# Dealing the second batch's side work at .56 of the feed-forward's work instead of .6 in the first sweep

## The chip, the core and the metric

One core of a Trainium2 chip runs the whole program. The engines named below are TensorE (PE, matmuls and transposes; PEld is its weight load), VectorE (DVE), ScalarE (ACT), GpSimd (POOL) and the SyncE queue (SP), which issues most transfers. The metric is the device time of one execution in microseconds (us), as the median of the runs shown.

## The reference

Attention on 8 batches of 12 heads, 448 tokens and 64 columns, then a spectral mixing of the 448 x 768 result, then a feed-forward network with 3072 hidden columns:

```python
q_n, k_n = (rmsnorm(q, g_q), rmsnorm(k, g_k))
scores = scale * np.matmul(q_n, k_n.transpose(0, 1, 3, 2))
attn = np.exp(scores - np.max(scores, axis=-1, keepdims=True))
attn = attn / (np.sum(attn, axis=-1, keepdims=True) + 1e-09)
x = np.matmul(attn, v)            # heads side by side: 448 x 768
mixed = np.real(np.fft.fft(np.fft.fft(x, axis=1), axis=2))
u = x + mixed
un = (u - mu) / np.sqrt(var + 1e-06)
out = u + np.maximum(un @ w_ch1, 0.0) @ w_ch2
```

The two weight matrices come in as 64-bit floating point numbers.

## The kernel before

The kernel makes 8 **sweeps**, one for each batch b. A sweep is the feed-forward of batch b, `ffn(b, ...)`, on TensorE: 24 pieces `up(m)` that make `h_m` (18 matmuls of 128x448 each, three passes on a high and a low half for precision), evacuated by ACT (high half) and DVE (low half) into `hs_m`, and 36 pieces `down(g, d)` that make `o_g_d` (12 matmuls each), added by DVE into `acc`. The order is `up(0)`, then for each group g of six four `up` and six `down`. The matmuls of both write to two banks of PSUM (`ffn`), so each piece waits until the piece two before it has been evacuated. It gives back its cost in nominal ns after each piece (3420 for an `up`, 2280 for a `down`).

While batch b is in the feed-forward, the **side work** of batch b+1 is dealt between the pieces: `aux(b + 1)`, a generator that gives attention (six head pairs: scores `S`, softmax `P`, transposes `pt`, products `av`), then the folds of its result for the Fourier transform (`fold`: DVE adds into `eo`, `sd`, `tot`), then `spectral`: matmuls `y`, evacuated to `Y`, matmuls `ab`, combined into `smdf`, then four token tiles, made in the order `un_0`, `un_2`, `un_1`, `un_3`: for each two groups of transposes (`x_000`, `x_001` for `un_0`, `x_010`, `x_011` for `un_2`, `x_10.` for `un_1`, `x_11.` for `un_3`; they take turns on two banks), a DVE pass to `u` with a sum `st`, an ACT pass to the centred rows `un` and an ACT pass that squares them (`xr`). At the start of the next sweep `ffn_input` transposes those four tiles into the six inputs `unT_0` to `unT_5` (PE transposes `un_p<-ident,un_i`, ACT high half, DVE low half), which `up(0)` needs.

`merge` sets how fast the side work is dealt:

```python
for cost in main:
    done += cost
    while side_done < done * ratio:
        x = next(side, None)
        ...
        side_done += x
```

with `RATIO = 0.49` in the sweeps from the second on and `RATIO_FIRST` in the first, where b is 0 and the side work is that of batch 1. The feed-forward of a sweep gives back 24 x 3420 + 36 x 2280 = 164160 in all.

The first sweep has a third load: the weights. There each piece's weights are loaded as 64-bit words (`dbl`), turned into two 32-bit halves by ACT, DVE and POOL (`mag`, lines 783 to 797, `w`, lines 802 and 803), and written back for the later sweeps, which only load them. A scheduler then sets the order of each engine's instructions from this program order and its own estimate of times; each engine runs its own list strictly in order.

Of the kernel before, what the change touches and what calls it, by code (L numbers as in the profile page):

```python
# [37 lines left out]


RATIO = 0.49  # L40
RATIO_FIRST = 0.6
CONVERT_EARLY = 0.12
EARLY = 2
DFT_STEP = 40
# [47 lines left out]
def spectral_block(ctx, tc, q, k, v, g_q, g_k, w1, w2, d1, d2, out, nb=B):  # L92
# [663 lines left out]
    def aux(b):  # L756

        EO, uns[b] = [], {}
        yield from attention(b, EO)
        yield from spectral(b, xTs[b], EO, uns[b])  # L760
# [368 lines left out]
    for b in range(nb):  # L1129
        merge(  # L1130
            ffn(b, ffn_input(b, uns.pop(b))),
            second if b == 0 else aux(b + 1) if b + 1 < nb else iter(()),
            RATIO if b else RATIO_FIRST,
        )
# [24 lines left out]
```

## Time and profile before

| | |
|---|---|
| time before, median of 3 runs | 2141.39 us (2141.15 to 2144.48) |
| profiled execution: time | 2144.78 us |
| profiled execution: span of the core | 2143.0 us |
| mean granted TensorE clock, of full speed | 0.984 |
| PE busy | 2074.9 us (97%) |
| DVE busy | 1548.4 us (72%) |
| ACT busy | 1023.3 us (48%) |
| POOL busy | 342.1 us (16%) |
| sweep 0, from its first matmul `h_0` | 177.0 us |
| sweep 1, from its first matmul `h_0` | 455.59 us |

The profiled execution took 3.39 us more than the median, so a sum of differences is made against its rows and then set on the median. Busy time of PE counts matmuls that overlap; what PE loses is read from its waits and from the granted clock, PEclk (1.00 is 2.4 GHz, 0.50 is 1.2 GHz). Sweep 0 runs from 177 to 455 us; before it stands the first batch's side work.

### The profile page before, as it was taken

Reading aid. Unit: us, or ns where it says so; the run is one execution under the profiler, and the core shown is the slowest. Engines: PE = TensorE matmul, PEld = TensorE weight load, DVE = VectorE, ACT = ScalarE, POOL = GpSimd, SP = SyncE. Lnnn points to the kernel's source line nnn. Section 1 sums busy time; section 2 is a strip of 40 time slices with the busy share of each in tenths; the row PEclk is TensorE's granted clock in tenths of the full one; section 3 lists DMA queues with packets and bytes.
Section 4 is the critical chain, followed back from the end, with each engine's and each line's share of the span. In section 5 each row is a group of like instructions: output and inputs, shape, how many; then the busy total and the mean of one; then the engine's idle time right before and its main releaser. Section 6 shows DMA issues by size and latency. Waiting matters only on the chain.

```text
span 2143.0 us, 31181 instructions
## 1 busy us (share of the span) xinstructions
PE 2074.9 (97%) x11256; PEld 1846.7 (86%) x11256; DVE 1548.4 (72%) x2948; ACT 1023.3 (48%) x2182; POOL 342.1 (16%) x182
## 2 busy tenths in 40 slices
PE   7877999999999999999999999999999999999998
PEld 4546888889999999999999999999999989999998
DVE  6788888977885878757886778858787578764122
ACT  6857876446542555335542455425553455422100
POOL 3324433311110101001110111101010011000000
PEclk9987999999999999999999999999999999999999
DMA  6538876776566855658555765667556674458874
GB/s 185 184 97 297 275 263 220 269 237 189 174 180 189 235 165 174 187 183 231 156 175 176 240 181 169 179 194 229 166 177 189 190 206 138 152 174 253 233 251 150
DMA packets 283550, 423.86 MB, mean 198 GB/s; under 512 B 181075, under 2 KB 200516, under 8 KB 283396
## 3 DMA queue, kind: packets, MB, share of 16 engines
q1 hardware_dynamic: 278962, 419.75, 63.8%
q10 hardware_dynamic: 4434, 2.11, 0.4%
q8 instruction: 90, 1.47, 0.3%
q14 instruction: 64, 0.52, 0.1%
HBM read 362.01 MB, written 65.31 MB: 199 GB/s over the span
## 4 chain that ended last, share of the span: by engine, by line
PE 81%; DVE 6%; DMA 5%; ACT 3%; issue 2%; POOL 1%; SPq 1%; DVEq 0%; POOLq 0%; ACTq 0%
PE h L1039 29%; PE o L1060 29%; PE S L409 5%; PE av L521 4%; PE pt L509 4%; DMA dbl<-w 2%; PE y L646 2%; PE qk L345 1%; DMA w<-w 1%; PE av L483 1%; DMA ur<-u_dram 1%; ACT P L115 1%; PE oT L996 1%; PE x L677 1%; PE un L908 1%
## 5 line engine op out<-in xcount | busy, mean ns | idle before, releaser
L1039 PE MATMUL h<-unT,w 128*128 128x448 f32 x3456 | 792.0, 372 | 3.4 <-DVE unT L115 1.4
L1060 PE MATMUL o<-hs,w 128*128 128x448 f32 x3456 | 786.4, 371 | 3.1 <-DVE acc L115 1.5
L1039 PEld LDWEIGHTS h<-unT,w 128*128 128x128 f32 x3456 | 638.9, 189 | 57.8 <-DVE unT L115 1.7
L1060 PEld LDWEIGHTS o<-hs,w 128*128 128x128 f32 x3456 | 635.9, 188 | 58.6 <-issue 3.4
L115 ACT ACTIVATE P<-S,mn 112x448 f32<-112x448 f32 x384 | 244.1, 638 | 232.6 <-DVE mn L115 226.7
L115 DVE TENSOR_REDUCE mn<-S 112x1 f32<-112x448 f32 x384 | 232.8, 616 | 47.9 <-PE S L409 38.3
L115 ACT ACTIVATE hs<-h 128x448 fp32r<-128x448 f32 x192 | 104.2, 543 | 299.0 <-PE h L1039 298.2
L115 DVE TENSOR_TENSOR acc<-o,acc 128x448 f32<-128x448 f32 (+1 forms) x240 | 146.9, 614 | 126.6 <-PE o L1060 125.0
L115 DVE SCALAR_TENSOR_TENSOR hs<-h,hs 128x448 fp32r<-128x448 f32 x192 | 119.0, 620 | 139.7 <-ACT hs L115 138.6
L115 POOL TENSOR_TENSOR qkn<-raw 112x1024 f32<-112x1024 f32 x36 | 68.6, 1904 | 679.3 <-PE qk L345 606.1
L115 POOL TENSOR_TENSOR ss<-ss,nhalf 112x16 f32<-112x16 f32 x48 | 142.6, 2972 | 190.2 <-DVE ss L115 167.2
L115 ACT CAST T<-pt 128x448 fp32r<-128x448 f32 x216 | 113.2, 532 | 107.3 <-PE pt L509 105.0
L521 PE MATMUL av<-T,vhl 128*128 128x448 f32 x432 | 151.0, 382 | 0.0
L115 DVE TENSOR_TENSOR T<-pt,T 128x448 fp32r<-128x448 f32 x216 | 131.4, 616 | 25.8 <-ACT T L115 24.7
L115 DVE TENSOR_SCALAR P<-P,sm 112x448 f32<-112x448 f32 x288 | 126.6, 479 | 3.8
L409 PE MATMUL S<-KD,QT 128*112 128x448 f32 x328 | 126.5, 386 | 0.6 <-ACT P L115 0.5
L509 PE MATMUL pt<-ident,P 112*128 112x112 f32 x864 | 124.8, 259 | 0.0
L409 PE MATMUL S<-rounded,QT 128*112 128x448 f32 x328 | 119.9, 366 | 0.0
L509 PEld LDWEIGHTS pt<-ident,P 112*128 112x128 f32 x864 | 103.5, 140 | 16.3 <-DVE R L115 0.3
L115 POOL TENSOR_TENSOR rstd<-st,nhalf 112x1 f32<-112x1 f32 (+2 forms) x32 | 20.2, 632 | 507.7 <-DVE st L115 507.7
L797 POOL TENSOR_TENSOR mag<-mag,dbl 128x768 uint32<-128x768 uint32 (+1 forms) x33 | 75.9, 2301 | 140.6 <-DVE mag L793 93.5
L521 PEld LDWEIGHTS av<-T,vhl 128*128 128x128 f32 x432 | 80.9, 188 | 8.3
(120 smaller groups left out, 2501.4 us busy)
## 6 DMA issues: line engine op xcount, KB each, us to landing
w<-w SPq DMA_DIRECT2D x192, 768.0 KB, 4.9
w<-w SPq DMA_DIRECT2D x288, 512.0 KB, 4.4
dbl<-w SPq DMA_DIRECT2D x20, 768.0 KB, 4.7
dbl<-w SPq DMA_DIRECT2D x13, 1024.0 KB
raw<-q SPq DMA_DIRECT2D x96, 112.0 KB, 3.8
raw<-k SPq DMA_DIRECT2D x96, 112.0 KB, 4.6
values<-v SPq DMA_DIRECT2D x96, 96.0 KB, 4.2
u_dram<-u SPq DMA_DIRECT2D x24, 336.0 KB, 3.8
```

The costliest lines, as they stand in the source:

```text
L115: ins = emit(*args, **kwargs)
L345: nc.tensor.transpose(pt[:, c * C : (c + 1) * C], qk[:, i, c].rearrange("t h d -> t (h d)"), ident[:C, :C],)
L409: ins = nc.tensor.matmul(s_, QT[:, h, cs], K[:, h], start=step == 0, stop=step == 1)
L483: nc.tensor.matmul(av[:, :S], vhl[:, 3 * h + j].rearrange("s h d -> s (h d)"), T, start=h + j == 0, stop=False,)
L509: nc.tensor.transpose(pt[:, c * C : (c + 1) * C], Pc[c][:, 512 * h + j * 128 : 512 * h + (j + 1) * 128], ident[:C, :C],)
L521: nc.tensor.matmul(av[:, :S], lv, T[:, i], start=(j == 0 and i == 0), stop=False)
L646: nc.tensor.matmul(o, src[:, par, t0 : t0 + n], D1[:, ri, par, cols], start=i != 1, stop=i != 0,)
L677: nc.tensor.transpose(xp[:n, i * 128 : (i + 1) * 128], src[:, 3 * half + i], ident)
L797: behind(nc.gpsimd.tensor_tensor(out=bits, in0=bits, in1=low, op=ALU.add))
L908: nc.tensor.transpose(pt[:, OFFS[i] : OFFS[i] + LENS[i]], uns[i][:, p * 128 : (p + 1) * 128], ident[: LENS[i], : LENS[i]],)
L1039: pace(nc.tensor.matmul(o, w[:, a, c], unT[c][:, z], start=n == 0, stop=n == 17))
L1060: pace(nc.tensor.matmul(o, w[:, a, f], hs[4 * g + f][:, z], start=n == 0, stop=n == 11))
```

## The change

One number: in the first sweep the second batch's side work is dealt until it has reached .56 of the feed-forward's work so far, instead of .6.

```diff
-RATIO_FIRST = 0.6
+RATIO_FIRST = 0.56
```

No instruction of arithmetic is added or taken away; what moves is the place of side work in the lists of the engines, between about 185 and 550 us of the trace. Three places show it.

**PE, at the end of sweep 0, before.** The rows are the transposes `x_110` and `x_111` (from the attention result `xT`) that start the last token tile, the `down` pieces `o_5_3` and `o_5_4`, and transposes of the feed-forward input (`un_1_4211<-ident,un_2_3932` is tile `un_2` for the input `unT_1`):

```order
L677 MATMUL x_110_4028<-ident,xT_1698 112x128 x3
L677 MATMUL x_111_4033<-ident,xT_1698 112x128 x3
L1060 MATMUL o_5_3_4155<-hs_23_4100,w_0_5_3_4022 128x448 x2
L908 MATMUL un_1_4211<-ident,un_1_3994 128x112
L908 MATMUL un_1_4211<-ident,un_2_3932 128x111
L908 MATMUL un_3_4227<-ident,un_1_3994 128x112
L908 MATMUL un_3_4227<-ident,un_2_3932 128x111
L1060 MATMUL o_5_4_4171<-hs_20_3707,w_0_5_4_4068 128x448 x3
```

A little further down the same list, the last `down` piece, the transposes of the last token tile, here `un_3_4040`, the next batch's scores and sweep 1's first matmul:

```order
L1060 MATMUL o_5_5_4187<-hs_21_4019,w_0_5_5_4103 128x448 x3
L1060 MATMUL o_5_5_4187<-hs_22_4065,w_0_5_5_4103 128x448 x3
L1060 MATMUL o_5_5_4187<-hs_23_4100,w_0_5_5_4103 128x448 x3
L908 MATMUL un_0_4203<-ident,un_3_4040 128x112
L908 MATMUL un_1_4211<-ident,un_3_4040 128x112
L908 MATMUL un_2_4219<-ident,un_3_4040 128x112
L908 MATMUL un_3_4227<-ident,un_3_4040 128x112
L409 MATMUL S_0_1_0_4312<-KD_0_3299,QT_0_3298 112x448
L409 MATMUL S_0_1_0_4312<-rounded,QT_0_3298 112x448
L409 MATMUL S_0_1_1_4313<-KD_0_3299,QT_0_3298 112x448
L409 MATMUL S_0_1_1_4313<-rounded,QT_0_3298 112x448
L1039 MATMUL h_0_4268<-unT_0_4208,w_1_0_4121 128x448
```

**The same place after the change**, from the last rows of `o_5_5` on; the transposes `x_100` to `x_111` that start the last two token tiles stand here:

```order
L1060 MATMUL o_5_5_4187<-hs_23_4045,w_0_5_5_4048 128x448 x3
L409 MATMUL S_0_0_0_4295<-KD_0_3353,QT_0_3352 112x448
L409 MATMUL S_0_0_0_4295<-rounded,QT_0_3352 112x448
L409 MATMUL S_0_0_1_4296<-KD_0_3353,QT_0_3352 112x448
L409 MATMUL S_0_0_1_4296<-rounded,QT_0_3352 112x448
L677 MATMUL x_100_4069<-ident,xr_1_4067 112x128 x3
L677 MATMUL x_101_4074<-ident,xr_1_4067 112x128 x3
L677 MATMUL x_110_4105<-ident,xT_1698 112x128 x3
L677 MATMUL x_111_4110<-ident,xT_1698 112x128 x3
L908 MATMUL un_0_4203<-ident,un_0_3999 128x113
L908 MATMUL un_0_4203<-ident,un_1_4081 128x112
L908 MATMUL un_0_4203<-ident,un_2_4020 128x111
```

and the rows that follow a little later, the transposes of the last token tile, now `un_3_4117`, up to sweep 1's first matmul:

```order
L908 MATMUL un_0_4203<-ident,un_3_4117 128x112
L908 MATMUL un_1_4211<-ident,un_3_4117 128x112
L908 MATMUL un_2_4219<-ident,un_3_4117 128x112
L908 MATMUL un_3_4227<-ident,un_3_4117 128x112
L409 MATMUL S_0_1_0_4312<-KD_0_3353,QT_0_3352 112x448
L409 MATMUL S_0_1_0_4312<-rounded,QT_0_3352 112x448
L409 MATMUL S_0_1_1_4313<-KD_0_3353,QT_0_3352 112x448
L409 MATMUL S_0_1_1_4313<-rounded,QT_0_3352 112x448
L1039 MATMUL h_0_4268<-unT_0_4208,w_1_0_4101 128x448
```

The `x_11.` transposes moved from the middle of `o_5_3` to behind `o_5_5`, and with them those of `x_10.`, which stood between `o_5_1` and `o_5_2`; between `x_111` and the transposes of the last tile `un_3` there were two whole `down` pieces (24 matmuls), and now there is none.

**PE, where the spectral part begins, before.** The matmuls `y` stood behind the first `down` of group 4:

```order
L1060 MATMUL o_4_0_3714<-hs_19_3648,w_0_4_0_3507 128x448 x3
L646 MATMUL y_0_0_3741<-D_76,eo_0_3408 113x2x65
L646 MATMUL y_0_1_3778<-D_76,eo_0_3408 112x2x65
L646 MATMUL y_1_0_3788<-D_76,eo_0_3408 113x2x65
L646 MATMUL y_1_1_3825<-D_76,eo_0_3408 112x2x65
L646 MATMUL y_0_0_3741<-D_76,eo_1_3579 113x2x65
```

After the change they stand behind `h_22`:

```order
L1039 MATMUL h_22_3933<-unT_5_1657,w_0_22_3731 128x448 x3
L646 MATMUL y_0_0_3840<-D_76,eo_0_3489 113x2x65
L646 MATMUL y_0_1_3877<-D_76,eo_0_3489 112x2x65
L646 MATMUL y_1_0_3913<-D_76,eo_0_3489 113x2x65
L646 MATMUL y_1_1_3923<-D_76,eo_0_3489 112x2x65
L646 MATMUL y_0_0_3840<-D_76,eo_1_3638 113x2x65
```

The first `y` matmuls moved past five `down` pieces and two `up` pieces; the first transposes of the first token tile (`un_0`), which stood just ahead of `h_23`, moved behind `o_5_3`.

**DVE, the third fold**, before. The rows are the fold of the last three head pairs (`eo_2`, `sd_2`, then into `eo_0`, `eo_1`, `tot`), with evacuations `hs` and weight conversion (`mag`, `w`) between:

```order
L115 TENSOR_TENSOR eo_2_3678<-xT_1698 128x449 x2
L115 TENSOR_TENSOR sd_2_3677<-eo_2_3678 128x2x225 x2
L115 TENSOR_TENSOR eo_2_3678<-sd_2_3677 128x4x113
L115 SCALAR_TENSOR_TENSOR hs_19_3648<-h_19_3629,hs_19_3648 128x448
L115 TENSOR_TENSOR eo_2_3678<-sd_2_3677 128x4x112
L803 TENSOR_TENSOR w_0_4_4_3651<-mag_4_4_3652,w_0_4_4_3651 128x512
L785 TENSOR_SCALAR mag_22_3766<-mag_22_3766 128x768
L115 SCALAR_TENSOR_TENSOR eo_0_3408<-eo_2_3678,eo_0_3408 128x900
L115 TENSOR_TENSOR eo_1_3579<-eo_1_3579,eo_2_3678 128x900
L115 TENSOR_TENSOR tot_3586<-tot_3586,eo_2_3678 128x900
```

and after the change, from its second step on, beside the evacuations of `o_4_4` and `o_4_5`:

```order
L115 TENSOR_TENSOR acc_1660<-o_4_4_3822,acc_1660 128x448
L803 TENSOR_TENSOR w_0_5_1_3836<-mag_5_0_3810,w_0_5_1_3836 128x512
L115 TENSOR_TENSOR sd_2_3757<-eo_2_3758 128x2x225 x2
L115 TENSOR_TENSOR acc_1660<-o_4_5_3850,acc_1660 128x448
L785 TENSOR_SCALAR mag_5_4_3956<-mag_5_4_3956 128x1024
L115 TENSOR_TENSOR eo_2_3758<-sd_2_3757 128x4x113
L115 TENSOR_TENSOR eo_2_3758<-sd_2_3757 128x4x112
L803 TENSOR_TENSOR w_0_5_2_3864<-mag_5_2_3865,w_0_5_2_3864 128x512
L789 TENSOR_SCALAR mag_5_4_3956<-mag_5_4_3956 128x1024
L115 SCALAR_TENSOR_TENSOR eo_0_3489<-eo_2_3758,eo_0_3489 128x900
L115 TENSOR_TENSOR eo_1_3638<-eo_1_3638,eo_2_3758 128x900
L115 TENSOR_TENSOR tot_3645<-tot_3645,eo_2_3758 128x900
```

The fold moved from `h_19` to the end of `down` group 4 and the start of `h_21`, and the last weights (`w_0_5_.`) are now converted between its steps.

## Rows read from the trace of the kernel before

**Rows 1.** Groups of the page: busy us, mean ns | idle us before.
```profile
L115 DVE TENSOR_REDUCE mn<-S 112x1 f32<-112x448 f32 x384 | 232.8, 616 | 47.9 <-PE S L409 38.3
...
L115 DVE TENSOR_SCALAR P<-P,sm 112x448 f32<-112x448 f32 x288 | 126.6, 479 | 3.8
```

**Rows 2.** Windows of sweep 0: length, busy us by engine, PEclk, DMA.
```profile
177.00:356.50 179.50, 175.65 (x892) 147.57 (x893) 152.52 (x226) 137.85 (x260) 70.29 (x35) 0.98 0.82 276
356.50:439.00 82.50, 76.30 (x395) 66.43 (x395) 79.85 (x111) 42.48 (x68) 31.05 (x14) 0.98 0.66 234
439.00:456.00 17.00, 17.00 (x99) 15.59 (x98) 9.72 (x28) 6.55 (x15) 1.31 (x3) 1.00 0.85 274
```

**Rows 3.** What PE waited for, 356 to 440: total us, times, longest.
```profile
PE un L908 <- ACT un L115: 2.3, 1, 2.3
PE y L646 <- DVE eo L115: 1.5, 1, 1.5
PE o L1060 <- DVE acc L115: 1.5, 1, 1.5
PE h L1039 <- DVE hs L115: 0.7, 1, 0.7
```

**Rows 4.** Windows of 2 us around the longest of these waits.
```profile
432.00:434.00 2.00, 2.00 (x8) 1.79 (x7) 2.00 (x2) 0.62 (x1) 1.29 (x1) 0.63 0.01 2
434.00:436.00 2.00, 2.00 (x7) 1.75 (x7) 2.00 (x8) 0.46 (x1) 0.55 (x1) 0.52 0.66 264
```

**Rows 5.** Timeline of PE, 399 to 456: start us, us, operation [idle before].
```profile
399.29 2.06 PE L646 MATMUL y<-D,eo 128*113 128x130 f32 x16 [1.52 <-DVE eo L115]
...
447.41 0.82 PE L677 MATMUL x<-ident,xT 128*112 128x128 f32 x6
...
455.59 0.37 PE L1039 MATMUL h<-unT,w 128*128 128x448 f32 x1
```

**Rows 6.** Timeline of ACT, 450 to 455.
```profile
450.07 0.94 ACT L115 ACTIVATE un<-u,st 112x768 f32<-112x768 f32 x1 [3.84 <-DVE st L115]
450.91 0.61 ACT L115 ACTIVATE P<-S,mn 112x448 f32<-112x448 f32 x1
...
451.52 0.62 ACT L115 ACTIVATE P<-S,mn 112x448 f32<-112x448 f32 x1
...
452.13 0.84 ACT L115 ACTIVATE xr<-un 112x768 f32<-112x768 f32 x1
...
454.69 1.84 ACT L115 CAST unT<-un 128x448 fp32r<-128x448 f32 x4 [1.62 <-PE un L908]
```

**Rows 7.** Timeline of DVE, 391 to 444.
```profile
391.90 2.24 DVE L115 TENSOR_TENSOR eo<-xT 128x449 f32<-128x449 f32 x2 [0.26 <-ACT xT L115]
...
400.07 1.09 DVE L115 TENSOR_TENSOR tot<-tot,eo 128x900 f32<-128x900 f32 x1
...
443.01 0.55 DVE L115 SCALAR_TENSOR_TENSOR u<-x,smdf 112x384 f32<-112x384 f32 x1
...
444.07 0.21 DVE L115 TENSOR_SCALAR st<-st 112x1 f32<-112x1 f32 x1
```

**Rows 8.** Timeline of PE where the first batch ends, ahead of sweep 0.
```profile
164.79 1.53 PE L677 MATMUL x<-ident,xr 128*112 128x128 f32 x6 [6.44 <-ACT xr L115]
...
181.73 1.79 PE L1039 MATMUL h<-unT,w 128*128 128x448 f32 x4
```

**Rows 9.** Groups of DVE by form, 340 to 460 us, columns as above.
```profile
L115 DVE TENSOR_TENSOR acc<-o,acc 128x448 f32<-128x448 f32 x18 | 11.1, 614 | 5.1 <-PE o L1060 5.0
L803 DVE TENSOR_TENSOR w<-mag,w 128x512 fp32r<-128x512 f32 x12 | 10.1, 854 | 0.0
L785 DVE TENSOR_SCALAR mag<-mag 128x1024 f32<-128x1024 f32 x5 | 8.1, 1615 | 1.3 <-ACT mag L783 1.3
...
L793 DVE SCALAR_TENSOR_TENSOR mag<-dbl,mag 128x1024 uint32<-128x1024 uint32 x5 | 6.1, 1216 | 0.0
...
L115 DVE SCALAR_TENSOR_TENSOR eo<-eo,eo 128x900 f32<-128x900 f32 x2 | 3.9, 1934 | 0.0
```

## The prediction, on record before the change was run

> **What bounds the kernel now.** I read the page first: PE is busy 97% of the span, so TensorE is the bound, and a change that adds no work can only give back, or take, what PE loses to waits and to a lower clock. The next view is the windows, because a mean over the span hides the stages. In sweep 0 there are three stages [rows 2]. From 177 to 356.5 us PE is busy 175.65 of 179.50 us, and I take its 3.85 us of loss as unchanged, since no engine is full there (DVE 152.52). From 356.5 to 439 us PE is busy 76.30 of 82.50, so 6.2 us are idle, while DVE is busy 79.85 of 82.50: DVE is the late engine here, since it has the folds and the last weights to do at once. From 439 to 456 us PE has no idle time at all. After 456 us PE is full, so what moves there costs nothing by itself.
>
> The waits say where the 6.2 us lie [rows 3]: 2.3 us for ACT's `un` (the first token tile), 1.5 for `eo` at the start of `y`, 1.5 for an `acc` that frees a bank, 0.7 for an `hs`, and a few tenths. A last loss is no wait: behind the 2.3 and the 0.7 us the granted clock is 0.63 and then 0.52, which is the lower level of 1.2 GHz most of the time, for two windows of 2 us [rows 4]. That is 2 x 0.37 + 2 x 0.48 = 1.7 us of full speed. So the stage that the change moves loses 6.2 + 1.7 = 7.9 us, 0.37% of the time. That is the most that it can win.
>
> **The change, part by part.** No instruction is added, so the sum has only waits in it. Three things move.
>
> *The first token tile.* Its transposes stood just ahead of `h_23`, and PE stood before them for 2.3 us, then 0.7 us for `hs`, then ran 1.7 us behind. After the change the first `x` transposes have `o_5_2` and much of `o_5_3` between them and the next, and `un_0` is wanted only behind `o_5_3`; by then DVE has no weight left to convert. From the `x` rows to `un_0`'s end the chain takes some 3 us (a `u` pair with 1.06 us to its `st`, 0.21 for it [rows 7], 0.94 for `un` [rows 6]), and two `down` pieces cover that. So this wait goes: -(2.3 + 0.7 + 1.7) = -4.7 us. Without that cover it would be at the 2.3 us that it is now.
>
> *The third fold and `y`.* Before, DVE needed from the first `eo_2` row at 391.90 to the end of `tot` at 400.07 + 1.09, so 9.3 us [rows 7], of which about 1.9 were other rows between. After the change more lies between: one L793 at 1.2, three `w` of 512 columns at 0.7 to 0.85, two `acc` at 0.61, one L785 at 0.7 to 1.6 [rows 9] and its L789, taken as a short L785. That is 6.3 to 7.5 us, so the fold takes 13.7 to 14.9. It starts about 1.5 us behind the end of `o_4_3` (an `acc` and a `w` go first). PE meanwhile has `o_4_4`, `o_4_5`, `h_21` and `h_22`, 60 matmuls at some 0.21 us, 12.7 us, and about 1.3 us of `y` that needs only `eo_0` and `eo_1` (sixteen such rows take 2.06 with their end [rows 5]). PE waits 15.2 to 16.4 less 14.0 = 1.2 to 2.4 us; I take 1.7, in place of the 1.5 for `eo` now. So +0.2. The 1.5 us for `acc` I leave as it is: DVE is as full there as before. The bounds: nothing is left of these waits, -3.0, or DVE's lateness only moves along, and the 4.7 us of the first tile come back at `y`, `h_21` or `h_23`.
>
> *The end of the sweep.* Before, `x_11.` stood in `o_5_3` and started at 447.41; `h_0` of sweep 1 came at 455.59 without a wait [rows 5], because 24 matmuls and other transposes lay between. Now nothing lies between but transposes. Let T be the start of `x_100`, right behind the four scores. DVE first takes the two minima of these scores, 0.62 each [rows 1], until about T + 0.9; then `u` for `un_1` and `st`, 1.06 + 0.21 [rows 7], to T + 2.2; ACT's `un_1`, 0.94, to T + 3.1, and its square, 0.84 with a read of about 0.1, to T + 4.1 [rows 6]. `x_110` has to wait for the bank of `x_100`, which `u` reads, but its own `u` is done by T + 3.5, so it isn't late. ACT then goes through `un_3`, two exponentials and a square: from 450.07 to 452.13 this took 2.06 us, and the square 0.94 more, so T + 7.1 [rows 6]. The first `unT` takes 0.5 (four in 1.84), T + 7.6, and `h_0` can start. Its second matmul and the next transposes need the low half from DVE, which stands behind two minima, two divisions at 0.48 [rows 1] and itself 0.61, counted from the second exponential at T + 6.2: T + 9.1. In these 9.1 us PE has 12 `x` and 14 `un` transposes at 0.08 to 0.1 and five matmuls at 0.2, 3.4 us. It loses 5.7 us. Queued behind are all of sweep 1's feed-forward, and nothing later can give that back, since PE is full there. The bounds: without the minima and with the `x` apart, the chain from 447.41 to the end of the square at 453.07 is 5.7 us, with 3.0 of PE work in it, a loss of 2.7; and where the first batch ends, the same steps with conversion between took from 164.79 to 181.73, 16.9 us [rows 8], of which PE's part at half speed is 6.8, a loss of 10.1. The row of 450 us is the nearer one, as DVE and ACT have no conversion left.
>
> *The clock there.* PE would be busy for little more than a third of these 9 us, in pieces. Behind 3.0 us of idle time in two pieces the clock fell and cost 1.7 us [rows 3, 4]; I take the same, +1.7, bounds 0 and 3.4 (twice). The Trainium skill, "TensorE: Matmul & The Clock Gate", section "Why this matters for your kernels", warns of long idle gaps between bursts of matmuls. No single gap that I expect is longer than the 2.3 us of now, so read alone the rule would leave the clock up and the sum would be 1.7 us lower; the trace shows that it fell behind such a gap, and the row decides.
>
> **The sum:** -4.7 + 0.2 + 5.7 + 1.7 = +2.9 us. On the profiled execution this is 2144.78 + 2.9 = 2147.7; that execution took 3.39 us more than the median of the runs shown, so on the median it is 2141.39 + 2.9 = 2144.3 us, +0.14%. About 0.2% (4.3 us) is what a measurement of this kernel can tell from no change.
>
> **The rivals.** *DVE stays late (slower).* The 7.9 us of the middle stage come from DVE's total work there, which is the same; the wait for `un` would only turn into one for `tot`, `hs_21` or `hs_23`. For it: DVE busy 97% of that stage [rows 2], and one `eo` row that takes 1.93 where others of its size take 1.09 [rows 7, 9]. Against it: the spectral part's own DVE rows leave the stage. Then +5.7 + 1.7 = +7.4, 2148.8 us. *The tail is covered (faster).* If DVE and ACT run the last tiles at the lower bound, 2.7 us with the clock up, and all 7.9 us of the middle go, the sum is -5.2: 2136.2 us. It decides from a loss of 3.6 us at the end of the sweep downwards. Against it: the list has no feed-forward matmul between `x_100` and `h_0`. *The clock stays up,* as by the page's rule: +1.2, 2142.6 us. *It does nothing to the time:* the moved rows find the same gaps elsewhere, 2141.4; the order speaks against it.
>
> **How the numbers follow.** Chances: the forecast 0.42, the clock that stays up 0.12, no effect 0.03, DVE that stays late 0.33, the covered tail 0.10. The first three lie within 0.2%: same 0.57, slower 0.33, faster 0.10. The forecast's own range is 2141 to 2145.5. The range for 8 in 10 runs from 2139.0 (half way into the covered tail) to 2150.0 (a little over the late DVE; above it lie the startup bound of 10.1 and a doubled clock loss).
>
> **What the profile after would show.** Right: a wait for `un` of about 1 us or less ahead of `h_23`, none there with a lower clock; a wait of PE for `eo` or `tot` behind `h_22`; behind `o_5_5` several waits of PE, for `un`, `unT` and `P`, of 5 to 6 us in all, with a granted clock below 1 in one or two windows of 2 us. Wrong: PE without a gap between `o_5_5` and `h_0`, or gaps of over 3 us between 360 and 440 us in new places, or a new loss in the first 180 us of sweep 0, such as a late weight (`w`) now that the lists of SP and POOL are in another order.

## The result, and the profile after

The kernel with .56 took 2162.8 us (median of 4 runs, 2160.92 to 2165.51) beside 2141.62 us for the kernel before in the same session: a ratio of 1.0097, 95% interval 1.008 to 1.0115. That is 21.2 us slower; I had forecast +2.9 us, with a range up to 2150.0.

The profiled execution of .56 took 2160.92 us, with a span of 2159.1 us: 16.1 us more than the span of before, while the medians are 21.2 apart, since the profiled execution of before took 3.2 us more than the 2141.62, and this one 1.9 less than its median. So stages are compared by what PE loses in each, and times by medians.

**How the loss of a stage is worked out**, here and for every kernel below: over windows of 2 us, the time in which PE isn't busy, and beside it the busy time multiplied by what the granted clock lacks of 1.00. The stages are the first one (195 to 360 us), the middle (360 to 448) and the end (448 to 490); 177 to 195 us loses 4 to 7 us in all kernels and is left out.

| us lost: idle + clock | first stage | middle | end |
|---|---|---|---|
| before | 1.5 + 0 | 6.2 + 1.7 | 0.3 + 0 |
| .56 | 6.9 + 0 | 8.1 + 3.8 | 3.8 + 4.3 |

The added losses, 5.4 + 4.0 + 7.8 us, with 0.7 from 177 to 195 us, make 17.9 us against the 16.1 of the spans; ahead of 177 and behind 490 us .56 loses some 2 us less than before. The clock's part shows in the windows of 2 us; the columns are the window, its length, PE busy (matmuls), PEclk, DMA share and GB/s:

```profile
427.00:429.00 2.00, 0.07 (x1) 1.00 0.72 298
429.00:431.00 2.00, 0.00 (x0) 0.69 0.08 31
431.00:433.00 2.00, 0.96 (x4) 0.50 0.63 262
433.00:435.00 2.00, 2.00 (x12) 0.50 0.00 0
435.00:437.00 2.00, 2.00 (x14) 0.60 0.55 229
...
469.00:471.00 2.00, 1.97 (x5) 0.50 0.13 51
471.00:473.00 2.00, 0.65 (x3) 0.50 0.00 0
```

Behind a wait of 5 us PE runs at the lower level, 1.2 GHz, for some 4.5 us more, and again among the waits at the end of the sweep.

PE's waits say what it stood for. The five longest of .56 from 195 to 360 us, in place of 1.2 us in three waits before; the columns are the line that waits, the engine and row that ended it, us in total, times, longest:

```profile
PE o L1060 <- DVE hs L115: 1.6, 1, 1.6
PE h L1039 <- DVE acc L115: 1.3, 1, 1.3
PE h L1039 <- ACT P L115: 1.2, 1, 1.2
PE av L483 <- ACT T L115: 0.9, 2, 0.6
PE S L409 <- ACT P L115: 0.9, 2, 0.6
```

And the five longest from 360 to 480 us, in place of [rows 3]:

```profile
PE y L646 <- DVE eo L115: 5.0, 1, 5.0
PE o L1060 <- DVE acc L115: 2.4, 1, 2.4
PE un L908 <- DVE unT L115: 1.4, 1, 1.4
PE un L908 <- DVE u L115: 1.3, 1, 1.3
PE un L908 <- ACT un L115: 0.9, 2, 0.7
```

The `un` wait of 2.3 us ahead of `h_23` is gone, as forecast; the one for `eo` is 5.0 us and not 1.7; `acc` is 2.4 and not 1.5; and there are several in the first stage, where I had expected no new ones.

**Two of them traced back.** ACT of .56 near 255 us (start, us, row, and in brackets the idle time ahead of it with what ended it):

```profile
254.55 0.18 ACT L115 ACTIVATION_READ_ACCUMULATOR P<-S,mn 112x1 f32 x1
258.91 1.14 ACT L784 ACTIVATE dbl<-dbl 128x1024 uint32<-128x1024 uint32 x1 [4.17 <-DMA dbl<-w]
259.94 0.54 ACT L115 ACTIVATE hs<-h 128x448 fp32r<-128x448 f32 x1
...
260.87 0.55 ACT L115 COPY xT<-av 128x448 f32<-128x448 f32 x1
261.30 0.63 ACT L115 ACTIVATE KD<-qk,gains 64x448 fp32r<-64x448 f32 x1
```

The same stretch of before:

```profile
255.28 0.56 ACT L115 CAST KD<-KD 64x448 fp32r<-64x448 f32 x1
255.75 0.52 ACT L115 COPY xT<-av 128x448 f32<-128x448 f32 x1
256.79 1.15 ACT L784 ACTIVATE dbl<-dbl 128x1024 uint32<-128x1024 uint32 x1 [0.52 <-DMA dbl<-w]
257.83 0.53 ACT L115 ACTIVATE hs<-h 128x448 fp32r<-128x448 f32 x1
```

Both wait for the load of weight `2_0`, which lands 2.1 us apart in the two traces. Before, the side work `KD` and `xT` stood ahead of the waiting row and filled the time; with .56 these rows stand behind it. `hs_8` stands right behind it in both lists: before, its matmuls ended at 255.8 us and the row began at 256.79; with .56 they ended at 254.5 and the row began at 258.91. PE then waits 1.57 us for `hs` at 261.20 us; that the small waits that follow come from the late `KD` and `P` is read from the order, not shown. The load is late by its issue for 1.0 us of the 2.1: SP's issue waits for a POOL row (`mag`, L797) that ended at 252.63 us, and at 251.60 before. The rest lies between issue and landing, and I have not traced it.

The same shape stands ahead of `y`. ACT and DVE of .56 at the third fold, rows chosen, in two fences:

```profile
416.76 1.13 ACT L783 ACTIVATE mag<-dbl 128x1024 f32<-128x1024 f32 x1 [3.36 <-DMA dbl<-w]
...
418.83 0.83 ACT L802 CAST w<-mag 128x768 fp32r<-128x768 f32 x1
419.56 0.20 ACT L115 COPY xT<-xT 128x1 f32<-128x1 f32 x1
```

```profile
415.07 0.62 DVE L115 TENSOR_TENSOR xT<-rt,xT 128x448 f32<-128x448 f32 x1
...
417.92 0.70 DVE L785 TENSOR_SCALAR mag<-mag 128x1024 f32<-128x1024 f32 x1 [1.70 <-ACT mag L783]
...
420.66 1.16 DVE L115 TENSOR_TENSOR eo<-xT 128x449 f32<-128x449 f32 x2
...
432.82 1.08 DVE L115 TENSOR_TENSOR tot<-tot,eo 128x900 f32<-128x900 f32 x1
```

`xT` is ready at 415.7 us, but its last column is copied by ACT behind a weight that waits 3.36 us for its load, and DVE's own row for that weight also stands ahead of the fold.

### The profile page after: what moved, and what is told of

Its sections match the earlier page's. It is cut to its first block, busy times and chain, and to the rows that moved or that the text cites. A ratio compares the mean times of both kernels' runs of the same rounds, so it can differ in the third digit from the quotient of the medians.

```text
span 2159.1 us, 31187 instructions
## 1 busy us (share of the span) xinstructions
PE 2077.7 (96%) x11256; PEld 1850.9 (86%) x11256; DVE 1553.4 (72%) x2948; ACT 1025.0 (47%) x2182; POOL 344.3 (16%) x182
## 4 chain that ended last, share of the span: by engine, by line
PE 84%; DVE 5%; DMA 3%; ACT 3%; issue 2%; POOL 1%; SPq 0%; DVEq 0%; ACTq 0%; POOLq 0%
PE o L1060 30%; PE h L1039 30%; PE S L409 6%; PE av L521 4%; PE pt L509 4%; PE y L646 2%; DMA dbl<-w 2%; PE qk L345 1%; PE av L483 1%; PE oT L996 1%; ACT P L115 1%; PE x L677 1%; PE un L908 1%; PE ab L725 1%; PE av L526 1%
## 5 line engine op out<-in xcount | busy, mean ns | idle before, releaser
L797 POOL TENSOR_TENSOR mag<-mag,dbl 128x768 uint32<-128x768 uint32 (+1 forms) x33 | 74.7, 2263 | 137.3 <-DVE mag L793 98.2
```

What stands on the lines that cost most here:

```text
L797: behind(nc.gpsimd.tensor_tensor(out=bits, in0=bits, in1=low, op=ALU.add))
```

## The experiments

The kernel before was run again beside each group of these kernels, with medians of 2141.18 to 2142.71 us, and the ratios are to those runs. A median of four runs is good to a few us, since the four lie 2 to 8 us apart.

**Two halves of the change.** In `merge` of the kernel before, the first sweep's limit `done * ratio` is replaced by a line through points (share of the feed-forward done, share dealt):

```diff
+        knots = [(0, 0), (0.6, 0.336), (0.7, 0.42), (1.01, 0.606)]
...
-            while side_done < done * ratio:
+            while side_done < (dealt(done) if ratio == RATIO_FIRST else done * ratio):
```

These are the points of early56; late56 has `[(0, 0), (0.5, 0.3), (0.6, 0.336), (1.01, 0.5656)]`.

> The side work is dealt at .56 until .6 of the first sweep's feed-forward, then quickly brought back to the .6 line, so that the last part has nearly the order of before. Theory (the loss has separate places): only the loss of the first stage stays. From 195 to 360 us PE stands still some 6.9 us as with .56 (1.5 before), ACT waits some 4 us for a weight near 255 us; no lower clock and under 1 us idle between the last down piece and h_0 of sweep 1; 2147 to 2149 us. Rival (the lateness of the first stage is carried on into the middle and the end): the middle and the end lose as with .56, over 2155 us.

Measured: 2153.84 us, ratio 1.006 (1.0045 to 1.0075), 12.7 us over before.

> The side work is dealt at .6 until half of the first sweep's feed-forward, then held back to the .56 line by .6 of it. Theory (separate places): the first stage loses what before loses (1.5 us idle from 195 to 330 us), the middle and the end lose what .56 loses there, some 4 and 8 us more than before: 2152 to 2155 us. Rival (the end is late only because the first stage was): 2141 to 2144 us.

Measured: 2149.88 us, ratio 1.0041 (1.0026 to 1.0056), 8.7 us over before. The two add to 21.4 us, the change's 21.2.

| us lost: idle + clock | first stage | middle | end |
|---|---|---|---|
| early56 | 6.5 + 0 | 8.1 + 3.1 | 0.4 + 0 |
| late56 | 1.1 + 0 | 5.9 + 2.3 | 4.5 + 4.0 |

The times of the halves do add, as the theory had it, but not in the sizes that it gave: I had expected 6 to 8 and 11 to 14 us. With the late half alone the middle loses 8.2 us, as much as before (7.9). What .56 adds in the middle belongs to the early half, which loses 11.2 us there and 0.4 at the end: of the rival the middle came true, and not the end. PE's waits of late56 from 360 to 448 us:

```profile
PE y L646 <- DVE eo L115: 4.9, 1, 4.9
PE o L1060 <- DVE acc L115: 0.9, 1, 0.9
```

**Other ratios.** One number each.

> One number, .58. In the order list the last token tile's transposes stand ahead of the last down piece here, with 24 transposes and 12 matmuls between them and h_0 of sweep 1. Theory: the end of the sweep loses under 2 us; what the other stages lose is set by their order, so 2140 to 2149 us. Rival (the loss grows evenly as the side work is dealt later): halfway, 2151 to 2153 us.

> One number, .62. Theory (each ratio gives another order, and which rows fall behind a load is not steered by the ratio; only the end is, and it is covered from .58 on): 2141 to 2150 us, with waits at other places than .6. Rival (.6 and .64 lie on an even curve): 2142 to 2145 us with the same places as .6.

> One number, .64: the side work ends at some 81% of the first sweep. Theory (the end already loses nothing at .6): the end can't win; DVE and ACT have the same work in a shorter time, so the stage from 195 to 400 us loses as much or more than before: 2141 to 2147 us. Rival (the later the side work, the longer, over the whole range): 2130 to 2138 us.

| | time, us | ratio (95%) | first stage | middle | end |
|---|---|---|---|---|---|
| .58 | 2155.4 | 1.0064 (1.0049 to 1.0079) | 7.4 + 0 | 6.3 + 1.7 | 2.0 + 0 |
| .62 | 2145.69 | 1.0015 (1.0006 to 1.0025) | 5.9 + 0 | 7.2 + 0 | 0 |
| .64 | 2146.35 | 1.0024 (1.0013 to 1.0036) | 3.9 + 0 | 5.4 + 3.1 | 0 |

The end came out nearly as expected: it loses 2.0 us at .58, the bound that I had given, and nothing from .62 on. .62 and .64 came out in the ranges of the theory. The time of .58 came out above both expectations: of the 7.7 us that it loses more than before in the three stages, 5.9 are in the first. The first stage loses 3.9 us or more at each ratio but .6; no even curve runs through it, as the theory has it.

**The end and the third fold.** cover56 orders a matmul of .56 behind the last transpose of `x_111`, foldfirst56 two weights behind the end of the fold, with the column copied by DVE; both56 has the two.

```diff
+                    if (b, g, d, n) == (0, 5, 4, 0):
+                        order(
+                            mm, lastx[1],
+                            mybir.DependencyClass.NoSync, mybir.DependencyReason.DATA,
+                        )
```

```diff
-            A.copy(xT[:, p, S : S + 1], xT[:, p, 0:1])
+            (V.tensor_copy if (b, p) == (1, 5) else A.copy)(
+                xT[:, p, S : S + 1], xT[:, p, 0:1]
+            )
...
+        if name in ("_0_5_2", "_0_5_4"):
+            order(
+                clamps[name], folded[0],
+                mybir.DependencyClass.NoSync, mybir.DependencyReason.DATA,
+            )
```

> As .56, but the first matmul of o_5_4 is ordered behind the last token tile's last transposes (x_111), so that two down pieces, 24 matmuls of 0.21 us, stand between x_111 and h_0 of sweep 1. Theory (the end loses because nothing covers the chain from x_100 to h_0): of the 8.0 us that .56 loses after 461 us (3.8 idle, 4.2 of clock) at most 1.5 are left, and 6 to 8 us less than .56: 2155 to 2157 us. Rival (x_100 itself comes late, or the end loses because DVE and ACT are behind anyway): the wait moves ahead of x_100 or stays at un, and the time stays within 2 us of .56, 2161 to 2164 us.

Measured: 2156.13 us, ratio 1.0064 (1.0049 to 1.0079), 6.7 us under .56. The end loses 2.9 us of idle time and no clock, beside 3.8 + 4.3. PE of cover56 from `o_5_4` on:

```profile
462.98 5.14 PE L1062 MATMUL o<-hs,w 128*128 128x448 f32 x24
467.95 1.54 PE L910 MATMUL un<-ident,un 113*128 113x113 f32 x14
...
470.15 0.37 PE L1041 MATMUL h<-unT,w 128*128 128x448 f32 x1
```

The 24 matmuls cover the chain, and `un` and `h_0` follow without a wait. The theory holds in its time and its place; it had at most 1.5 us left at the end, and 2.9 are. What is left of waits (1.1 us for `bs` ahead of the scores, 0.5 and 0.8 ahead of `x`, 0.5 behind `h_0`) is the rival's, and small.

> As .56, but the last column of xT, which the third fold reads, is copied by DVE instead of ACT, and the conversion of the weights 5_2 and 5_4 on DVE is ordered behind that fold. Theory (y waits because rows that wait for a weight's load stand ahead of the fold in ACT's and DVE's lists): the fold starts at some 416 us instead of 420.7, PE waits less than 1 us for eo instead of 5.0, and the lower clock behind it (2.3 us) goes too: 6 to 7.5 us less than .56, 2155 to 2157 us. Rival (DVE is simply full there, the wait is its total work): the wait moves to h_23 or to o_5_2's weights, within 2 us of .56.

Measured: 2159.76 us, ratio 1.0085 (1.0068 to 1.0102), 3.0 us under .56. DVE, and then PE, of foldfirst56:

```profile
414.19 2.45 DVE L115 TENSOR_TENSOR eo<-xT 128x449 f32<-128x449 f32 x2
...
424.72 1.09 DVE L115 TENSOR_TENSOR tot<-tot,eo 128x900 f32<-128x900 f32 x1
```

```profile
426.19 1.27 PE L650 MATMUL y<-D,eo 128*113 128x130 f32 x10
```

The fold starts 6.5 us earlier and `y` waits for nothing, so this wait was one of order. But the middle as a whole loses 7.8 us and not the 4.6 that would be left of 11.9 without the 7.3 of `y`: 1.1 us for `ab` came in its place, and between 365 and 390 us, where the rows still stand in the order of .56, this execution lost 6.8 us (2.9 for `acc`, 2.2 for `av`, 1.7 of clock) where the one of .56 lost 4.8. That much one execution can differ from another in one stage. The end of this execution lost 10.3 us, 8.1 with .56. So 3.0 us lie between the theory's 6 to 7.5 and the rival's 2.

> As .56 with both orders of the kernels on the fold and on the last token tile: the third fold ahead of weights 5_2 and 5_4, and o_5_4 behind x_111. Theory (the places add): what the two gave alone, 3.0 and 6.7 us, is taken off .56 together: 2152 to 2154 us, no wait for eo, none over 1 us behind o_5_3; what is left over .6 is the first stage and 365 to 385 us. Rival (what is won at one place comes back at the other): 2156 us or more.

Measured: 2152.29 us, ratio 1.0048 (1.003 to 1.0067), 10.5 us under .56, where the two alone give 3.0 + 6.7 = 9.7. The sizes fit, but loosely: two of the four runs took 2148.2 and 2148.6 us, two 2156.0 and 2156.2, and the median lies between. PE waits for no `eo`; it still loses 10.6 us in the middle, and 1.5 us in one wait for `smdf` at the end, where I had none over 1 us.

**What waits behind a load.** hs8_56 orders ACT's row of one weight of .56 behind `hs_8`. hs21_60 does the like in the kernel before, for three rows of weight `5_4`:

```diff
+        if name == "_0_2_0":
+            order(
+                low_half, highs[8],
+                mybir.DependencyClass.NoSync, mybir.DependencyReason.DATA,
+            )
```

```diff
+        if name == "_0_5_4":
+            for ins, before in zip((first, second, third), (evacuated[-2][0], evacuated[-2][0], evacuated[-2][1])):
```

unlate60 moves the transposes of sweep 1's input instead, and hsall_60 has that edit and the one of hs21_60 for every weight:

```diff
+                if b == 1:
+                    order(
+                        ins, paced[-1 - 72],
+                        mybir.DependencyClass.NoSync, mybir.DependencyReason.DATA,
+                    )
```

> As .56, but ACT's scaling of weight 2_0 (the row that waits 4.2 us for its load at 254.7 us) is ordered behind the evacuation hs_8. The lists from about 310 us on come out in another order, so only the stretch from 195 to 300 us is to be read. Theory (rows that could go stand in ACT's list behind a row that waits for a load): hs_8 goes at 254.8 us, the wait of PE for hs (1.6 us) goes, and of the 4.0 us that .56 loses from 195 to 300 us 1.6 to 2.5 go; what side work still stands behind the load keeps its waits. Rival (the later waits, for KD, T and P, have other causes and grow): 4 us stay lost.

Measured: 2156.42 us in one run. The row of the load still waits 2.9 us, with `hs_8` now ahead of it. ACT of hs8_56:

```profile
253.85 0.54 ACT L115 ACTIVATE hs<-h 128x448 fp32r<-128x448 f32 x1
254.29 0.61 ACT L810 CAST w<-mag 128x512 fp32r<-128x512 f32 x1
257.83 1.15 ACT L786 ACTIVATE dbl<-dbl 128x1024 uint32<-128x1024 uint32 x1 [2.93 <-DMA dbl<-w]
```

From 195 to 300 us PE stands still 2.5 us beside 4.0 with .56, and not at all between 255 and 263 us. The theory holds; the 1.5 us that went are a little less than the least that it gave, 1.6, in one execution.

> The kernel before (.6) with one thing changed: the transposes of sweep 1's input that stand ahead of h_23 are ordered behind h_23. Theory (the term of my sum that the first token tile's wait alone costs 2.3 + 0.7 of waits and 1.7 of clock): 4.7 us less than before, 2136 to 2138 us, no wait for un, no lower clock near 433 us. Rival (DVE and ACT are late there anyway): the wait turns into one for hs_22 or hs_23 ahead of h_23 or o_5_0, and the time stays within 1.5 us of before.

Measured: 2142.74 us, ratio 1.0 (0.999 to 1.0009). It comes out as the rival had it. The two longest of PE's waits of unlate60 from 360 to 490 us:

```profile
PE h L1044 <- DVE hs L115: 3.4, 1, 3.4
PE o L1065 <- DVE acc L115: 1.5, 1, 1.5
```

The transposes are out of the way, and `h_23` waits 3.4 us for an evacuation instead of 2.3 + 0.7. It is that of `h_21`, whose bank `h_23` takes, and it came as late in the kernel before. ACT, and then DVE, of before:

```profile
425.06 1.16 ACT L783 ACTIVATE mag<-dbl 128x1024 f32<-128x1024 f32 x1 [3.52 <-DMA dbl<-w]
...
428.18 0.54 ACT L115 ACTIVATE hs<-h 128x448 fp32r<-128x448 f32 x1
```

```profile
430.55 0.62 DVE L115 SCALAR_TENSOR_TENSOR hs<-h,hs 128x448 fp32r<-128x448 f32 x1
```

The matmuls of `h_21` end some 5 us ahead of ACT's row, which stands behind the load of weight `5_4`. The wait for `un` hid the one for `hs_21`.

> The kernel before (.6) with the conversion of weight 5_4 (its two ACT rows and its first DVE row) ordered behind the evacuation hs_21 on both engines. Theory (what waits ahead of h_23 is hs_21, which stands in ACT's and DVE's lists behind the load of weight 5_4): hs_21 is evacuated at 423 to 425 us instead of 428 to 431, the waits of 3.0 us ahead of h_23 and the lower clock behind them (1.7 to 3 us) go: 2136 to 2138 us. Rival (DVE has too much work between 418 and 436 us, whatever its order): the wait comes back as one for hs_22, acc or w within the next 25 us; within 1.5 us of before.

Measured: 2140.33 us, ratio 0.9996 (0.9987 to 1.0004). The wait for `hs` ahead of `h_23` is 1.8 us, with 0.9 more ahead of `o`, and no lower clock. Most of the waits came back, as many as the rival had; what went is the clock's part. Its reason, that DVE has too much work whatever its order, is not shown, since `hs_21` did not go at 423 to 425 us. ACT of hs21_60:

```profile
428.03 0.62 ACT L813 CAST w<-mag 128x512 fp32r<-128x512 f32 x1 [5.97 <-POOL mag L808]
428.55 0.54 ACT L115 ACTIVATE hs<-h 128x448 fp32r<-128x448 f32 x1
```

With the load's rows gone, `hs_21` stands behind another row of a weight, which waits 5.97 us for POOL, and comes no earlier than before.

> The kernel before (.6) with the same rule for each of the weights that are converted in the first sweep (ACT's two rows and DVE's first behind the evacuation of the up piece before the last), and the transposes of sweep 1's input that stood ahead of h_23 behind it. Theory (ready evacuations standing behind a load are the main loss of the sweep): of the 14 us that before loses from 177 to 490 us 5 to 7 go, 2135 to 2138 us. Rival (the weights then come late themselves, or other rows wait in their place): 2140 us or more.

Measured: 2146.11 us, ratio 1.0016 (1.0007 to 1.0025). The first stage loses 0.6 us, the least but one of all kernels; the middle 13.9. That is 0.9 us won and 6.0 lost: the rival, since other rows wait in their place (4.1 us of PE's waits there are for `hs`). Whether a full DVE is the reason is not shown.

**POOL.** sq56 and sqb56 let ACT make one square that POOL makes in .56; three56 adds the edit of sq56 to both56; best60 and best60b add that of sq56 and that of sqb56 to hs21_60. The pair is `(2, 0)` in sq56 and `(2, 1)` in sqb56:

```diff
-        if b < EARLY:
+        if b < EARLY or (b, p) == (2, 0):
             A.activation(sq, flat, AF.Square)
```

> As .56, with one row moved between engines: the square of batch 2's first pair (qkn, 4.06 us on POOL from 367.75 us) is made by ACT. Theory (a DVE row that starts while a POOL row runs ends only with it: the sums row at 369.99 us takes 4.21 us instead of 0.17, and acc stands behind it): the wait for acc at 372 us falls from 2.4 to under 1 us and no lower clock follows it (1.7 us): 3 to 4.5 us less than .56, 2158 to 2160 us. Rival (DVE is late there by its own work): the wait stays over 2 us and the time within 2 us of .56.

Measured: 2160.9 us, ratio 1.0085 (1.0072 to 1.0099). It moved a square that ran elsewhere, so it doesn't test the theory, and the `acc` wait stayed (2.1 us).

> As .56, with the square of batch 2's second pair on ACT (the one that POOL makes at 367.75 us; sq56 had moved the first pair's, which stood at 326 us, and the row of 4.7 us came back behind two POOL rows in a chain). Theory (DVE's row is held as long as POOL rows follow each other): only L797 is left there, no DVE row between 365 and 378 us takes over 2.5 us, the wait for acc falls from 2.4 to under 1.3 us without a lower clock behind it: 2.5 to 4 us less than .56, 2159 to 2160.5 us. Rival (DVE is late by its own work): the wait and the clock stay, within 2 us of .56.

Measured: 2162.37 us, ratio 1.0095 (1.0081 to 1.0108). The `acc` wait at 372 us is gone with its lower clock, and 8 us later PE waits 3.4 us for another `acc`, with 1.5 of clock. The place is explained; the time isn't won, as the rival had it.

> As .56 with the three orders together: the square on ACT, the third fold ahead of weights 5_2 and 5_4, o_5_4 behind x_111. Theory: what the two gave together (10.5 us) and 3 to 4 us more are taken off .56, 2148 to 2150 us; left over .6 is the first stage, 5 to 7 us. Rival: the two alone are all there is to win, 2152 us or more.

Measured: 2149.32 us, ratio 1.0033 (1.0021 to 1.0045): as expected in size, but by luck: the square in it is the one of sq56, and the `acc` wait that it was to take away stayed (2.1 us). It loses 4.8 us in the first stage and 10.4 behind it, where before loses 1.5 and 8.2.

> The kernel before (.6) with two of these: weight 5_4 behind hs_21 and the square of batch 2's first pair on ACT. Theory (less of DVE's time is lost to POOL, and DVE is what is late from 356 to 439 us): the 6.2 us that PE stands still there fall to 3 or 4, and the lower clock goes: 2137 to 2139 us. Rival (hs21_60's result is the floor): 2140 to 2142 us.

Measured: 2142.5 us, ratio 1.0002 (0.9993 to 1.001): no difference that can be told, near the rival's 2140 to 2142 us and above the theory's range.

> The kernel before (.6) with weight 5_4 behind hs_21 and the square of batch 2's second pair on ACT. Theory (DVE is late from 356 to 439 us, and every us that POOL takes from it there counts): 1 to 3 us under before, 2138 to 2140.5 us. Rival: no difference that can be told from before, 2140.5 to 2142.5 us.

Measured: 2139.77 us, ratio 0.9992 (0.9983 to 1.0001), with 0.4, 5.3 and 0 us lost in the three stages. This is in the theory's range. It has the lowest median of all, 2.1 us under before, but its interval still reaches 1, so a gain isn't shown.

## Why the prediction was wrong

**The step that failed most: "I take its 3.85 us of loss as unchanged, since no engine is full there".** The first stage lost 5.4 us more, and its order reached into the middle: early56 alone costs 12.7 of the 21.2 us. A full engine is not needed. An engine that runs its list in order stands still with ready work behind a row that waits for a load, and ACT, 47% busy over the span of .56, did so for 4.17 us (0.52 before). Dealing the side work later moved rows that had filled this wait behind it, and the load itself came 2.1 us later. Eight kernels that start with the order of .56 (.56, early56, cover56, foldfirst56, both56, sqb56, sq56 and three56) lose 4.8 to 7.9 us in this stage, six that start with that of .6 (before, late56, unlate60, hs21_60, best60 and best60b) 0.4 to 2.1. hs8_56 shows the mechanism for one wait of 1.6 us; that all the others in the stage are of that kind is not shown, so the cause of most of the 5.4 us stays open. A new loss in this stage was one of my own signs of being wrong.

**"-4.7" for the first token tile failed.** The wait for `un` did go, but unlate60 takes it away by itself and wins nothing: it had hidden a wait for `hs_21`, which ends at 431.17 us in the kernel before and at 431.55 in unlate60. So its 2.3 us were no term of their own, and neither was the clock behind them. With .56 that wait is gone too, and the one ahead of `y` took its place. My rival "DVE stays late", which I gave 0.33, had the size for the late half of the change: 2148.8 us by its sum, 2149.88 measured in late56. Its reason, DVE's total work, isn't shown: foldfirst56 took the wait ahead of `y` away by order alone, and of the nearly 8 us from the matmuls of `h_21` to the end of `hs_21` some 5 pass before ACT's row starts.

**"+0.2" for the third fold failed by its start.** Its length came out near, 13.7 to 14.9 us forecast and 13.2 measured (420.66 to 433.90); the rows that I put between its steps add up to 5.9 to 7.3 us and not to 6.3 to 7.5, which makes it 13.3 to 14.7. I had it start 1.5 us behind the end of `o_4_3`; it started some 6 us behind it, 5.0 behind the end of the `xT` row that it needs, with rows of weights in front. Over before, `y` costs 3.5 us of wait and 2.3 of clock more. **"The 1.5 us for acc I leave as it is"** failed too: 2.4 us and 1.7 of clock, behind a DVE row that POOL held up (below).

**The end of the sweep was right in its chain, and in its sum partly by luck.** Forecast 5.7 + 1.7 = 7.4 us, measured 3.8 + 4.3 = 8.1: two errors of opposite sign. PE of .56 there:

```profile
462.33 0.82 PE L677 MATMUL x<-ident,xr 128*112 128x128 f32 x6
...
470.51 0.74 PE L1039 MATMUL h<-unT,w 128*128 128x448 f32 x1
472.60 0.98 PE L908 MATMUL un<-ident,un 113*128 113x113 f32 x4 [1.35 <-DVE unT L115]
```

With T at 462.33, `h_0` starts at T + 8.2 and the next transposes at T + 10.3, where I had T + 7.6 and T + 9.1. Less of it was idle and more was clock, since PE worked through most of the chain at a granted clock of 0.50 to 0.57. The price of the clock was too small everywhere: with .56 it is 8.1 us in the middle and at the end, and I had 1.7.

The trace shows the granted clock at 0.53 and 0.61 (375 to 379 us) behind the single wait of 2.4 us for `acc`, and at 0.54 and 0.61 (293 to 297 us) behind one of 2.2 in foldfirst56. It stayed at 1.00 behind one of 2.4 in .62 and behind one of 2.9 in foldfirst56 (369 to 373 us). So in these runs the length of a single wait doesn't tell whether the clock falls. "TensorE: Matmul & The Clock Gate" of the Trainium skill, section "Why this matters for your kernels", warns of long gaps between bursts. The rival that I had drawn from it, a clock that stays up, did not come about: the trace agrees with the warning behind the 5.0 us ahead of `y`, and shows falls behind shorter gaps as well.

**The sum, as it should have stood:** 5.4 in the first stage, 4.0 in the middle, 7.8 at the end.

## What to carry to other kernels

Where a scheduler orders lists that engines run strictly in order, one number that moves side work can reorder what waits for loads, and a stage without a full engine isn't safe from it: read, for each engine, what stands ready behind a row that waits for a DMA or for another engine. Taking away the wait that shows can uncover the next one (unlate60, sqb56); of the single edits here, covering a chain won most (cover56). Before a term is booked as a gain, ask what else the waiting row needs, and when that comes.

## What the hardware showed that I had not expected

DVE rows took longer while POOL worked. DVE, and then POOL, of .56:

```profile
369.99 4.21 DVE L115 TENSOR_SCALAR sums<-sums 112x8 f32<-112x8 f32 x1
374.11 0.61 DVE L115 TENSOR_TENSOR acc<-o,acc 128x448 f32<-128x448 f32 x1
```

```profile
367.75 4.06 POOL L115 TENSOR_TENSOR qkn<-raw 112x1024 f32<-112x1024 f32 x1 [0.83 <-PE qk L345]
371.77 2.39 POOL L797 TENSOR_TENSOR mag<-mag,dbl 128x1024 uint32<-128x1024 uint32 x1
```

A row of 8 columns, 0.16 us in sqb56, ends with the second of two POOL rows in a chain, 4.21 us after it began, and the `acc` behind it is what PE waits for. From 180 to 460 us of .56 there are 22 DVE entries of the timeline that take at least 0.3 us more than the shortest of their form. All overlap a POOL row, and together they lose 31 us; before loses 28, best60 23. "SBUF — State Buffer" of the Trainium skill, section "Who interferes with whom", has it: the two share a pair of ports, and where both need it the one that comes second waits for the whole instruction of the other. The trace agrees, and adds that two POOL rows in a chain hold DVE through both, here and in sq56 (4.76 us behind rows of 2.43 and 2.27). Whether less work on POOL makes the kernel faster is open: best60b points that way, within what can be told from no change.
